# Keys, queries and x of two chunks in one tile, turned by one DMA transpose, and v loaded from SyncE's queue

## The chip, the core and the metric

The kernel runs on one core of a Trainium2 chip. The metric is the device time of one execution in microseconds (us); the median over 13 runs before the change is 304.58 us. A core has a matrix engine (TensorE, "PE" in the profile; its weight loads are listed as "PEld"), VectorE ("DVE"), ScalarE ("ACT"), GpSimd ("POOL") and SyncE ("SP"). Each engine works through its own instruction stream in order, and semaphores between the streams make one wait for another. SyncE computes nothing: its stream issues transfers. An issue is itself an instruction in a stream, so whatever stands behind a waiting issue waits too.

## The reference

```python
# q, k, v: (8 sequences, 8 heads, 576 positions, 64), float32
scores = scale * np.matmul(q, k.transpose(0, 1, 3, 2))
rel = pos[:, None] - pos[None, :]
mask = (rel >= 0) & (rel < 64)              # a causal window of 64 keys
scores = np.where(mask, scores, -1000000000.0)
attn = softmax(scores)                      # shortened here
x = np.matmul(attn, v)                      # then laid out as (4608 tokens, 512)
h = np.maximum(x @ w_in, 0.0)               # w_in: 512 x 2048
out = h * h @ w_out                         # w_out: 2048 x 512, out: 4608 x 512
```

Attention within a short window comes first, and a two-layer network with a squared ReLU follows it. Nearly all the arithmetic is in the two large products.

## The kernel before

**Tiles.** The 4608 tokens are 36 chunks of 128 tokens, and chunks 2p and 2p+1 are pair p. A sequence of 576 positions is two pairs of 256 and a rest of 64. The rests of all sequences are gathered in pairs 8 and 15 (`TAILS`): each of their four chunks holds the last 64 queries of two sequences, and needs 128 keys and values of each. Four chunks are a group g of 512 tokens, and there are nine groups.

**One chunk's way.** Rows of k, q and v are loaded as float32 into staging tiles (`fetch_rows`, L122), cast to float16 (`cast_k`, `cast_q`, `cast_v`, mostly on POOL, L264; the tails' at L301 and L304), and the keys and queries are turned so that the head dimension lies across partitions. The first 14 chunks are turned by PE (`T`, L330) and copied out of PSUM; from chunk 14 on SyncE issues a DMA transpose for each (`dma_kT` L357, `dma_tail` L363, `dma_qT` L368). `S_` (L388) makes the scores with the turned keys as weights, `expo` (L394) the exponential on ScalarE, `keep` (L399) the mask on DVE, `V` (L411) the product with v, and `norm` (L418, L419) divides by the row sum and writes x. x is turned too, by PE for groups 0 to 3 (`X`, L430), and by a DMA transpose of each chunk after that (`dma_xT`, L438).

The keys of a pair lie in one tile of 64 + 256 columns: a block of 64 query rows needs the 64 keys before it as well, so `halo` (L315, L317) has DVE fill the first 64 columns, with zeros at the start of a sequence or with the last 64 columns of the pair before.

**The network.** `UP(g, f)` (L489) makes one of 16 slices of h for a group; ScalarE takes the ReLU (L493), and either ScalarE (L496) or DVE (L499) squares it. There are two PSUM banks for these slices. `out_seven(g)` (L577) makes the second product with seven half-size products in place of eight; its half sums and differences are made by DVE (`hsum`, L565), its results leave PSUM at L592 to L599, and SyncE stores them (L608, L614).

**Order.** The first phase, some 80 us, is a list written by hand (`FIRST`). After it a loop runs over g = 2 to 9. Each turn puts the second product of group g-1, the first product of group g, the attention of group g+1 and the loads into one list with a time from 0 to 1 each, and issues them in the order of these times. In `loads`, a pair a = 2g+3 is turned from 0.06 on (its second chunk at 0.11), its halo is filled at 0.2, and the chunks two further on are loaded at 0.14 and 0.38; the second pair follows 0.46 later in the same way. `attention` has scores at 0.02 and 0.48, the product with v at 0.25 and 0.71, and the turning of x at 0.275 and 0.735.

**Queues.** All loads, stores and transposes are issued from SyncE, except for the v loads of chunks from `AHEAD` = 22 on, which are issued from ScalarE's stream (16 loads):

```python
fetch_rows(vv[:, n], v, b + n, S - 128, eng=nc.scalar if i >= AHEAD else nc.sync)
```

In the built program the transfers share eight completion counters, taken in turn, and an issue waits until the transfer eight places earlier has landed, whichever queue issued that one.

**Staging.** `two_tiles` hands out six tiles of two chunks each. A key and a query load of one chunk share one such tile; from chunk 22 on two v loads share one. POOL's casts free them. The float16 copies rotate through seven one-chunk tiles each for keys and queries, the turned queries through five, x through three.

Of the kernel before, what the change touches and what calls it, by code (L numbers as in the profile page):

```python
# [41 lines left out]
def kernel(  # L42
# [13 lines left out]
    P = 128  # L56
# [15 lines left out]
    st16 = ctx.enter_context(tc.tile_pool(name="st16", bufs=7))  # L72
# [66 lines left out]
    AHEAD = 22  # L139
# [4 lines left out]
    def fetch_kq(i, eng=nc.sync):  # L144
        st = two_tiles()
        sts["k", i], sts["q", i] = st[:, 0], st[:, 1]
        for nm, src in (("k", k), ("q", q)):
            fetch_rows(sts[nm, i], src, *place(i), eng=eng)

    def fetch_v(i, eng=nc.sync):  # L150
        if i < AHEAD:
            sts["v", i] = stage.tile([P, H, D], FP32, name="v_st", tag="st", bufs=5)
        elif i % 2 == 0:
            vv = two_tiles()
            sts["v", i], sts["v", i + 1] = vv[:, 0], vv[:, 1]
        fetch_rows(sts["v", i], v, *place(i), eng=eng)

    def fetch_tail(i):

        kk, vv = two_tiles(), two_tiles()  # L160
        if i % 2 == 0:
            qq = two_tiles()
            sts["q", i], sts["q", i + 1] = qq[:, 0], qq[:, 1]
        sts["k", i], sts["v", i] = (kk[:, 0], kk[:, 1]), (vv[:, 0], vv[:, 1])
        b = tail_seq(i)
        for n in range(2):
            fetch_rows(kk[:, n], k, b + n, S - 128)
        for n in range(2):
            fetch_rows(sts["q", i], q, b + n, S - 64, 64, 64 * n)
        for n in range(2):  # L170
            fetch_rows(vv[:, n], v, b + n, S - 128, eng=nc.scalar if i >= AHEAD else nc.sync)
# [80 lines left out]
    for name, m in (("minus_first", mask_first), ("minus_inner", mask_inner)):  # L252
        minus.append(const.tile([P, 512], FP16, name=name))
        nc.vector.tensor_scalar(out=minus[-1][:], in0=m[:].rearrange("p a r -> p (a r)"),
                                scalar1=-BIG, scalar2=None, op0=ALU.add)


    kTs, qTs, pms, xs, xTs = {}, {}, {}, {}, {}
# [8 lines left out]

    def cast_k(i, eng=nc.gpsimd):
        k16s[i] = st16.tile([P, H, D], FP16, name="k16", tag="k16")
        copy(eng, k16s[i][:], sts["k", i])  # L270

    def cast_q(i, eng=nc.gpsimd):
        q16s[i] = st16.tile([P, H, D], FP16, name="q16", tag="q16")
        copy(eng, q16s[i][:], sts["q", i])
# [18 lines left out]
    def xT_of(g):  # L293
        if g not in xTs:
            xTs[g] = xtp.tile([P, DMC, 512], FP16, name="xT", tag="xT")
        return xTs[g]

    def cast_tail(i):
        k16s[i] = [st16.tile([P, H, D], FP16, name="k16", tag="k16") for _ in range(2)]
        for n in range(2):  # L300
            nc.gpsimd.tensor_copy(out=k16s[i][n][:], in_=sts["k", i][n])  # L301
        cast_q(i)
        for n, vv in enumerate((v_ods, v_evs)):
            nc.gpsimd.tensor_copy(out=vv[i % NV][:, :, 0:D], in_=sts["v", i][n])  # L304

    def kT_of(p):

        if p not in kTs:
            kTs[p] = attw.tile([P, HP, 64 + 2 * P], FP16, name="kT", tag="kT", bufs=4)
        return kTs[p]  # L310

    def halo(i):
        p = i // 2
        if is_first(i):
            nc.vector.memset(kT_of(p)[:, :, 0:64], 0.0)  # L315
        else:
            nc.vector.tensor_copy(out=kT_of(p)[:, :, 0:64], in_=kT_of(p - 1)[:, :, 2 * P:2 * P + 64])  # L317

# [5 lines left out]
    def T(p):  # L324
        ps = att_bank("qkT_ps")[:].rearrange("p s f -> p (s f)").bitcast(FP16).rearrange(
            "p (s two a t) -> p s a two t", s=2, two=2, a=HP)
        for s, src in enumerate((k16s, q16s)):
            for n in range(2):
                for hp in range(HP):
                    nc.tensor.transpose(out=ps[:, s, hp, n, :],  # L330
                                        in_=src[2 * p + n][:, 2 * hp:2 * hp + 2, :],
# [6 lines left out]

    def q_cols(i):
        qTs[i] = attw.tile([P, HP, P], FP16, name="qT", tag="qT", bufs=5)  # L340
        return qTs[i][:]
# [14 lines left out]
    def dma_kT(i):  # L356
        nc.sync.dma_start_transpose(out=k_cols(i), in_=k16s[i][:].rearrange("p h d -> p (h d)"))  # L357

    def dma_tail(i):

        kTs["tail", i] = attw.tile([P, HP, 64 + 2 * P], FP16, name="kT", tag="kT", bufs=4)
        for n in range(2):
            nc.sync.dma_start_transpose(out=kTs["tail", i][:, :, n * P:(n + 1) * P],  # L363
                                        in_=k16s[i][n][:].rearrange("p h d -> p (h d)"))
        dma_qT(i)

    def dma_qT(i):
        nc.sync.dma_start_transpose(out=q_cols(i), in_=q16s[i][:].rearrange("p h d -> p (h d)"))  # L368

    def S_(i):  # L370
        sc = att_bank("sc")
        scv = sc[:].rearrange("p a (h b t) -> p a h b t", h=HP, b=2)
        for a in range(2 if i < 4 else 0):
            nc.tensor.matmul(sc[:, a, :], ident[:], minus[i > 0][:], start=True, stop=False,
                             skip_group_check=True)
        tail = is_tail(i)
        kT = kTs["tail", i] if tail else kT_of(i // 2)
        for hp in range(HP):
            for blk in range(2):
                for hh in range(2):  # L380
                    r0 = 64 * hh
                    k0 = P * blk if tail else i % 2 * P + 64 * blk
                    qT = qTs[i][r0:r0 + 64, hp, :]
# [4 lines left out]
                    nc.tensor.matmul(scv[:, hh, hp, blk, :], kT[r0:r0 + 64, hp, k0:k0 + P], qT,  # L388
# [26 lines left out]
    def norm(i):  # L415
        xs[i] = attw.tile([P, 2, HP, D], FP16, name="x_sb", tag="x_sb")
# [3 lines left out]
            out=xs[i][:], in0=avs[i][:, :, :, 0:D],  # L420
            in1=rden[:].to_broadcast([P, 2, 4, D]), op=ALU.mult)

    def xT_cols(i):
        return xT_of(i // 4)[:, :, (i % 4) * P:(i % 4 + 1) * P]

    def X(i):
        xps[i] = att_bank("xt_ps")[:, 0, :].bitcast(FP16)[:, 0:DMC * P].rearrange(
            "p (c t) -> p c t", c=DMC)
        for c in range(DMC):
            nc.tensor.transpose(out=xps[i][:, c, :],  # L430
                                in_=xs[i][:, c // 2, 2 * (c % 2):2 * (c % 2) + 2, :],
# [5 lines left out]
    def dma_xT(i):  # L437
        nc.sync.dma_start_transpose(out=xT_cols(i), in_=xs[i][:].rearrange("p a h d -> p (a h d)"))  # L438
# [16 lines left out]
    def U(p, j):  # L455
        t0 = p % 2 * 256
        pool, tag = either_pool()
        hps = pool.tile([P, 2, 256], FP32, name="hps2", tag=tag)
        for f in range(2):
            for c in range(DMC):  # L460
                nc.tensor.matmul(  # L461
                    hps[:, f, :], w_in_sb[:, c, (2 * j + f) * P:(2 * j + f + 1) * P],
                    xT_of(p // 2)[:, c, t0:t0 + 256], start=(c == 0), stop=(c == DMC - 1))
# [22 lines left out]
    def UP(g, f):  # L486
        hps = ps_up.tile([P, 512], FP32, name="hps", tag="ps_u")
        for c in range(DMC):
            nc.tensor.matmul(  # L489
                hps[:], w_in_sb[:, c, f * P:(f + 1) * P], xT_of(g)[:, c, :],  # L490
# [57 lines left out]
    def out_seven(g):  # L548
# [115 lines left out]
        "T": T, "ck": copy_kT, "cq": copy_qT, "tk": dma_kT, "tq": dma_qT, "h": halo,  # L664
        "S": S_, "e": expo, "ea": lambda i: expo(i, lo), "eb": lambda i: expo(i, hi),
        "m": keep, "ma": lambda i: keep(i, lo), "mb": lambda i: keep(i, hi),
        "V": V, "n": norm, "X": X, "x": copy_xT, "dx": dma_xT,
# [11 lines left out]
    def attention(g):  # L679
# [10 lines left out]
        def to_xT(i):  # L690
# [4 lines left out]
            else:  # L695
                dma_xT(i)
# [6 lines left out]
        for h in range(2):  # L703
# [3 lines left out]
                   (t + dx, lambda a=a: to_xT(a)), (t + dx + 0.001, lambda b=b: to_xT(b))]  # L707
        return ev

    def load(i):  # L710
        if is_tail(i):
            fetch_tail(i)
            cast_tail(i)
            return
        fetch_kq(i)
        fetch_v(i, nc.scalar if i >= AHEAD else nc.sync)
        cast_k(i)
        cast_q(i)
        cast_v(i)
        shift_v(i)  # L720

    def loads(c):

        ev = []
        for h in range(2):
            t = 0.46 * h
            for n in range(2):
                i = c + 2 * h + n
                if i < NCK:
                    ev.append((t + 0.06 + 0.05 * n, lambda i=i: dma_tail(i) if is_tail(i)  # L730
                               else (dma_kT(i), dma_qT(i))))
                if i < NCK and n == 0 and not is_tail(i):
                    ev.append((t + 0.2, lambda i=i: halo(i)))
                if i + 2 < NCK:
                    ev.append((t + 0.14 + 0.24 * n, lambda i=i: load(i + 2)))
# [5 lines left out]
    for g in range(2, NTB + 1):  # L741
# [6 lines left out]
        if g + 1 < NTB:  # L748
            ev += attention(g + 1)
            ev += loads(4 * g + 6)  # L750
# [34 lines left out]
```

## Time and profile before

| | |
|---|---|
| median of 13 runs | 304.58 us (303.31 to 306.59) |
| the profiled execution | 304.58 us |
| its span in the profile | 302.9 us |
| DMA busy, mean data rate | most of the time up to about 240 us; 190 GB/s |
| granted TensorE clock | 1.00 in every stretch looked at |

| group of instructions | count | mean |
|---|---|---|
| `UP` matmuls, 128x512 (L489) | 448 | 379 ns |
| ReLU of these on ScalarE (L493) | 112 | 597 ns |
| half sums and differences of h on DVE (L565) | 64 | 681 to 844 ns |
| casts of k, q on POOL (L264) | 40 | 729 to 757 ns |
| key transposes by DMA, landing after issue (L357, L363) | 26 | 3.8 us, median |
| query transposes by DMA (L368) | 22 | 2.6 us, median |
| x transposes by DMA (L438) | 20 | 4.0 us, median |
| k loads of one chunk, 256 KB | 26 | 4.2 us, median |

The profile shows one execution. Its span runs from the first instruction to the last. Matmuls overlap in PE's pipeline and their ends are modelled, so the time that PE takes for a matmul is the distance from one start to the next, which is shorter than the mean in the table: four matmuls of 512 columns start over 0.87 us. In lines of the timeline, the columns are the start in us, the time from the first start to the last end in us, the engine, the source line, the operation, what it writes and reads, the count, and in brackets how long the engine had been idle and what was seen to release it. "SPq" and "ACTq" are issues of transfers from the streams of SyncE and ScalarE.

### The profile page before, as it was taken

How to read it: one execution, taken by the hardware profiler on the slowest of the kernel's cores; microseconds unless marked ns; L12 is line 12 of the kernel's file. 1: busy time of each engine (PE TensorE's matmuls, PEld its weight loads, DVE VectorE, ACT ScalarE, POOL GpSimd, SP SyncE). 2: the span in 40 equal slices, each digit the busy share in tenths (PEclk: the TensorE clock that was granted, in tenths of full speed). 3: DMA queues.
4: the chain of work that ended last, by engine and by line, in shares of the span. 5: the costliest groups of instructions: out<-in, count | busy, mean ns of one | idle time of the engine just before them, and what ended most of it. 6: DMA issues, size and time to landing. Idle time of an engine off the chain costs nothing.

```text
span 302.9 us, 7559 instructions
## 1 busy us (share of the span) xinstructions
PE 285.6 (94%) x3026; PEld 197.1 (65%) x3026; DVE 214.5 (71%) x398; ACT 186.4 (62%) x303; POOL 121.4 (40%) x176
## 2 busy tenths in 40 slices
PE   1989999999999999999999999998989999999995
PEld 0658888855566676666666666665656666666685
DVE  4668888866878569775968596766575967646493
ACT  3558799795584756756675667475637675566510
POOL 1338955674605419263744566334263400000000
DMA  8999999896359779999997999999999911400133
GB/s 229 308 394 265 275 292 370 279 233 159 124 119 214 159 192 243 156 196 213 255 196 166 273 208 171 225 242 191 174 181 248 173 34 28 147 0 0 71 105 106
DMA packets 152931, 57.65 MB, mean 190 GB/s; under 512 B 129344, under 2 KB 144704, under 8 KB 152896
## 3 DMA queue, kind: packets, MB, share of 16 engines
q1 hardware_dynamic: 136256, 52.97, 72.1%
q10 hardware_dynamic: 16640, 4.20, 7.4%
q8 instruction: 24, 0.39, 0.5%
q14 instruction: 11, 0.09, 0.1%
HBM read 38.80 MB, written 9.44 MB: 159 GB/s over the span
## 4 chain that ended last, share of the span: by engine, by line
PE 64%; DVE 11%; DMA 10%; ACT 5%; SPq 4%; issue 3%; POOL 2%; ACTq 0%; POOLq 0%; DVEq 0%
PE hps L489 20%; PE hps L461 9%; PE opsC L577 7%; PE opsD L577 6%; DMA kq_st<-in_k_dram 6%; DVE hs_all L565 5%; PE ops L537 4%; PE opsB L577 3%; PE sc L388 3%; PE opsA L577 3%; DVE pm L399 3%; PE av L411 2%; PE qkT_ps L330 2%; ACT pm L394 2%; ACT hrelu L493 2%
## 5 line engine op out<-in xcount | busy, mean ns | idle before, releaser
L489 PE MATMUL hps<-xT,w_in_sb 128*128 128x512 f16 x448 | 112.9, 379 | 4.9 <-ACT hrelu L493 2.5
L493 ACT ACTIVATE hrelu<-hps 128x512 f32<-128x512 f32 x112 | 66.3, 597 | 73.9 <-PE hps L489 65.6
L577 PEld LDWEIGHTS <-h 128*128 128x128 f16 x624 | 60.4, 98 | 21.0 <-issue 0.2
L489 PEld LDWEIGHTS <-w_in_sb 128*128 128x128 f16 x448 | 42.8, 98 | 37.9 <-issue 5.4
L499 DVE SCALAR_TENSOR_TENSOR h<-hps,hrelu 128x512 f16<-128x512 f32 x56 | 38.6, 689 | 37.8 <-ACT hrelu L493 37.7
L264 POOL COPY v_od<-v_ev 64x512 f16<-64x512 f16 x52 | 36.6, 704 | 8.8 <-ACT v_ev L262 5.8
L394 ACT ACTIVATE pm<-sc 128x1024 f16<-128x1024 f32 (+1 forms) x40 | 35.6, 936 | 4.1 <-PE sc L388 3.9
L496 ACT ACTIVATE h<-hrelu 128x512 f16<-128x512 f32 x56 | 35.2, 629 | 1.6
L264 POOL CAST k<-kq_st 128x512 f16<-128x512 f32 x18 | 13.6, 757 | 48.2 <-DMA kq_st<-in_k_dram 47.9
L577 PE MATMUL opsA<-w_out_sb,h 128*128 128x256 f16 x240 | 31.0, 273 | 0.0
L577 PE MATMUL opsD<-wb_all,h 128*128 128x256 f16 x240 | 31.0, 273 | 0.0
L577 PEld LDWEIGHTS <-hs_all 128*128 128x128 f16 x256 | 25.0, 98 | 8.6
L461 PE MATMUL hps<-xT,w_in_sb 128*128 128x256 f16 x256 | 30.4, 273 | 0.0
L461 PEld LDWEIGHTS <-w_in_sb 128*128 128x128 f16 x256 | 24.1, 98 | 3.2 <-DVE w_in_sb L266 0.2
L419 DVE TENSOR_TENSOR x_sb<-av,rden 128x512 f16<-128x512 f32 x36 | 24.9, 691 | 1.2
L399 DVE TENSOR_TENSOR pm<-pm,mask_inner 128x1024 f16<-128x1024 f16 x25 | 19.8, 791 | 5.7 <-ACT pm L394 5.6
L264 POOL CAST q<-kq_st 128x512 f16<-128x512 f32 x22 | 16.0, 729 | 9.4 <-DMA kq_st<-in_q_dram 9.2
L388 PEld LDWEIGHTS <-kT 64*128 64x128 f16 x576 | 12.7, 95 | 7.6 <-issue 6.1
L577 PE MATMUL opsC<-w_out_sb,h 128*128 128x256 f16 x128 | 16.4, 273 | 0.0
L577 PE MATMUL opsC<-w_out_sb,hs_all 128*128 128x256 f16 x128 | 16.4, 273 | 0.0
L577 PE MATMUL opsB<-wb_all,hs_all 128*128 128x256 f16 x128 | 16.4, 272 | 0.0
L388 PE MATMUL sc<-qT,kT 64*128 64x64 f16 x576 | 15.9, 203 | 0.4 <-DVE qT L264 0.4
(97 smaller groups left out, 363.4 us busy)
## 6 DMA issues: line engine op xcount, KB each, us to landing
kq_st<-in_k_dram SPq DMA_DIRECT2D x26, 256.0 KB, 4.2
out_dram<-osb_all SPq DMA_DIRECT2D x12, 512.0 KB, 4.0
v_st<-in_v_dram SPq DMA_DIRECT2D x20, 256.0 KB, 4.9
kq_st<-in_q_dram SPq DMA_DIRECT2D x18, 256.0 KB, 4.3
kq_st<-in_v_dram ACTq DMA_DIRECT2D x16, 256.0 KB, 4.4
k_st<-in_k_dram SPq DMA_DIRECT2D x7, 512.0 KB, 5.4
q_st<-in_q_dram SPq DMA_DIRECT2D x7, 512.0 KB, 5.9
out_dram<-osb_all SPq DMA_DIRECT2D x11, 256.0 KB, 2.2
```

Of the source, the lines that this page charges most:

```text
L264: eng.tensor_copy(out=out, in_=in_)
L388: nc.tensor.matmul(scv[:, hh, hp, blk, :], kT[r0:r0 + 64, hp, k0:k0 + P], qT, start=i >= 4, stop=True, skip_group_check=i < 4)
L394: nc.scalar.activation(out=pms[i][:, part], in_=scs[i][:, part], func=AF.Exp, scale=1.0 / float(D) ** 0.5)
L399: nc.vector.tensor_tensor(out=pms[i][:, part], in0=pms[i][:, part], in1=mask[:].rearrange("p (o a) r -> p o (a r)", o=1) .to_broadcast([P, ...
L419: nc.vector.tensor_tensor(out=xs[i][:], in0=avs[i][:, :, :, 0:D], in1=rden[:].to_broadcast([P, 2, 4, D]), op=ALU.mult)
L461: nc.tensor.matmul(hps[:, f, :], w_in_sb[:, c, (2 * j + f) * P:(2 * j + f + 1) * P], xT_of(p // 2)[:, c, t0:t0 + 256], start=(c == 0), sto ...
L489: nc.tensor.matmul(hps[:], w_in_sb[:, c, f * P:(f + 1) * P], xT_of(g)[:, c, :], start=(c == 0), stop=(c == DMC - 1))
L493: nc.scalar.activation(out=hrelu[:], in_=hps[:], func=AF.Relu)
L496: later(2 if f == 0 else 0, lambda: nc.scalar.activation(out=h2_of(g)[:, f, :], in_=hrelu[:], func=AF.Square))
L499: nc.vector.scalar_tensor_tensor(out=h2_of(g)[:, f, :], in0=hps[:], scalar=0.0, in1=hrelu[:], op0=ALU.max, op1=ALU.mult)
L565: nc.vector.tensor_tensor(out=Sh[i][:, ks], in0=x[:, ks], in1=y[:, ks], op=op)
L577: nc.tensor.matmul(rows_of(bank, m), a[:, kk, m * P:(m + 1) * P], w[:, kk], start=(first and kk == 0 and (m == 0 or bank in apart)), stop= ...
```

## The change

All pairs from 7 on (`AHEAD` is now 7, counted in pairs) are handled as a whole. The float16 keys of a pair lie in one tile of two chunks, and so do its queries and its x; each of the three is turned by one DMA transpose of 1024 columns in place of two of 512. The staging tiles hold two chunks of one kind (k, q or v), and a pair's six loads (twelve for a tail pair) are issued one after the other at 0.14 and at 0.60 of a group, all from SyncE. The casts follow in the order k, k, q, q, v, v.

Since the transpose fills the turned tile from its first column, the keys have no room for the halo in front of them. `halo_apart`, at 0.30 and 0.76, has DVE build a second tile of 128 columns: the last 64 keys of the pair before (or zeros), and the first 64 of the pair itself. The first block of queries takes its keys from there.

x of a group is stored with the chunk outside and the column inside, so a matmul of `UP` reads its 512 columns as four runs of 128. The two constant masks `minus` now lie in an output tile that is not in use yet.

```diff
-    st16 = ctx.enter_context(tc.tile_pool(name="st16", bufs=7))
+    st16 = ctx.enter_context(tc.tile_pool(name="st16", bufs=3))
...
-    AHEAD = 22
+    AHEAD = 7
...
+    def fetch_two(nm, p):
+        src = {"k": k, "q": q, "v": v}[nm]
+        st = two_tiles()
+        b, s0 = place(2 * p)
         for n in range(2):
+            fetch_rows(st[:, n], src, b, s0 + n * P)
+        for n in range(2):
+            sts[nm, 2 * p + n] = st[:, n]
...
+    def halo_apart(p):
+        khs[p] = attw.tile([P, HP, P], FP16, name="kh", tag="kh", bufs=2)
+        if is_first(2 * p):
+            nc.vector.memset(khs[p][:, :, 0:64], 0.0)
+        else:
+            c0 = 2 * P if p - 1 < AHEAD else 2 * P - 64
+            nc.vector.tensor_copy(out=khs[p][:, :, 0:64], in_=kT_of(p - 1)[:, :, c0:c0 + 64])
+        nc.vector.tensor_copy(out=khs[p][:, :, 64:P], in_=kT_of(p)[:, :, 0:64])
...
-    def dma_kT(i):
-        nc.sync.dma_start_transpose(out=k_cols(i), in_=k16s[i][:].rearrange("p h d -> p (h d)"))
...
+    def dma_k(p):
+        if p in TAILS:
+            for i in (2 * p, 2 * p + 1):
+                kTs["tail", i] = attw.tile([P, 2, HP, P], FP16, name="kT", tag="kT", bufs=4)
+                flip(kTs["tail", i][:].rearrange("p n a t -> p (n a) t"),
+                     k16s["tail", i][:].rearrange("p n h d -> p (n h d)"))
+        else:
+            flip(kT_of(p)[:].rearrange("p a (n t) -> p (a n) t", n=2),
+                 k16s[p][:].rearrange("p n h d -> p (n h d)"))
+
+    def dma_q(p):
+        flip(qT_of(p)[:].rearrange("p n a t -> p (n a) t"),
+             q16s[p][:].rearrange("p n h d -> p (n h d)"))
...
-    def dma_xT(i):
-        nc.sync.dma_start_transpose(out=xT_cols(i), in_=xs[i][:].rearrange("p a h d -> p (a h d)"))
+    def dma_xT(p):
+        nc.sync.dma_start_transpose(
+            out=xT_of(p // 2)[:, p % 2 * 2:p % 2 * 2 + 2].rearrange("p n c t -> p (n c) t"),
+            in_=xs[p][:].rearrange("p n a h d -> p (n a h d)"))
...
-                hps[:], w_in_sb[:, c, f * P:(f + 1) * P], xT_of(g)[:, c, :],
+                hps[:], w_in_sb[:, c, f * P:(f + 1) * P], xT_of(g)[:, :, c, :],
...
+    def load(p):
+        if p in TAILS:
+            fetch_tail(p)
+        else:
+            for nm in "kqv":
+                fetch_two(nm, p)
+        for i in (2 * p, 2 * p + 1):
...
+                cast_k(i)
+        for i in (2 * p, 2 * p + 1):
+            cast_q(i)
...
-                if i + 2 < NCK:
-                    ev.append((t + 0.14 + 0.24 * n, lambda i=i: load(i + 2)))
+            t, a = 0.46 * h, p + h
+            if a < NCK // 2:
+                ev.append((t + 0.06, lambda a=a: (dma_k(a), dma_q(a))))
+                if a not in TAILS:
+                    ev.append((t + 0.3, lambda a=a: halo_apart(a)))
+            if a + 1 < NCK // 2:
+                ev.append((t + 0.14, lambda a=a: load(a + 1)))
```

## The prediction

> **What bounds the kernel now.** I read the page's busy times first, then the waits, then the timelines of PE, ScalarE and SyncE around the longest gaps. The page shows PE full and full speed granted:
>
> ```profile
> PE 285.6 (94%) x3026; PEld 197.1 (65%) x3026; DVE 214.5 (71%) x398; ACT 186.4 (62%) x303; POOL 121.4 (40%) x176
> ```
>
> So only what keeps PE from its next matmul counts. The timeline of PE, from 80 us on, has these gaps over 0.1 us (start, length, instruction, and in brackets the gap before it and its releaser):
>
> ```profile
> 102.78 1.02 PE L489 MATMUL hps<-xT,w_in_sb 128*128 128x512 f16 x4 [0.45 <-DVE h L499]
> ...
> 119.93 1.89 PE L489 MATMUL hps<-xT,w_in_sb 128*128 128x512 f16 x8 [0.60 <-DVE h L499]
> 133.86 1.02 PE L489 MATMUL hps<-xT,w_in_sb 128*128 128x512 f16 x4 [0.31 <-ACT hrelu L493]
> ...
> 178.53 1.89 PE L489 MATMUL hps<-xT,w_in_sb 128*128 128x512 f16 x8 [0.19 <-DVE h L499]
> ...
> 209.27 1.02 PE L489 MATMUL hps<-xT,w_in_sb 128*128 128x512 f16 x4 [0.84 <-ACT hrelu L493]
> 211.63 1.02 PE L489 MATMUL hps<-xT,w_in_sb 128*128 128x512 f16 x4 [0.46 <-DVE h L499]
> 219.58 1.89 PE L489 MATMUL hps<-xT,w_in_sb 128*128 128x512 f16 x8 [0.17 <-DVE h L499]
> 224.35 1.02 PE L489 MATMUL hps<-xT,w_in_sb 128*128 128x512 f16 x4 [1.38 <-ACT hrelu L493]
> ...
> 240.03 1.89 PE L489 MATMUL hps<-xT,w_in_sb 128*128 128x512 f16 x8 [0.31 <-DVE h L499]
> ```
>
> Five of them (0.31, 0.84, 0.46, 0.17, 1.38) make 3.16 us. The distance between the first opsA matmuls of successive groups agrees. They start at 112.44, 142.34, 171.45, 200.58, 232.83 and 261.40, so groups 3 to 7 take 29.90, 29.11, 29.13, 32.25 and 28.57 us (the last one starts a group without scores, 0.57 us, so 29.14 like for like). Group 6 is 3.1 us over the floor, group 3 is 0.8.
>
> What happens there is in the timeline of ScalarE, whose own queue issues the v loads (ACTq) between the ReLUs:
>
> ```profile
> 132.24 0.44 ACTq L122 DMA_DIRECT2D kq_st<-in_v_dram  x1
> 132.73 1.08 ACT L493 ACTIVATE hrelu<-hps 128x512 f32<-128x512 f32 x2 [1.98 <-DMA kq_st<-in_q_dram]
> ...
> 208.15 0.38 ACTq L122 DMA_DIRECT2D kq_st<-in_v_dram  x1
> 208.62 0.60 ACT L493 ACTIVATE hrelu<-hps 128x512 f32<-128x512 f32 x1 [3.62 <-PE hps L489]
> ...
> 214.76 0.37 ACTq L122 DMA_DIRECT2D kq_st<-in_v_dram  x1
> 215.23 0.60 ACT L493 ACTIVATE hrelu<-hps 128x512 f32<-128x512 f32 x1 [1.95 <-DVE u L599]
> ...
> 222.80 0.37 ACTq L122 DMA_DIRECT2D kq_st<-in_v_dram  x1
> 223.22 1.09 ACT L493 ACTIVATE hrelu<-hps 128x512 f32<-128x512 f32 x2 [3.26 <-DMA kT<-k]
> ```
>
> Each long ACT idle (1.98, 3.62, 1.95, 3.26) ends just after a v load goes out. The load waits, and the ReLU behind it waits too: in the built program a v load on ScalarE's queue waits for its staging tile and for the completion counter of the DMA eight places earlier, often a transpose that SyncE has yet to issue. The name in the bracket is only the last event seen; the 3.26 us one names such a transpose. A late ReLU frees its PSUM bank late and makes the square behind it late, and PE, with two such banks, stops.
>
> **The change, part by part.**
>
> *v loads leave ScalarE* (16 issues). The four blocks go, and with them the five gaps: -3.2 us. Group 6's excess (3.1) plus group 3's 0.31 would say 3.45; the listed gaps are the lower count and I take -3.3. Here the Trainium skill speaks against the change: "DMA: Bandwidth & Descriptors", section "Issuing engines are not separate DMA queues", says that spreading issues over engines only saves sequencer time for the issue, a small thing. By that rule the move gains ScalarE some 16 x 0.4 us of issue under cover and costs SyncE as much: about 0 in the sum, 304.6. The row differs: the issue takes 0.37 to 0.44 us, but it also waits in order, up to 3.62 us. The measurement decides.
>
> *SyncE's queue*, per steady group. Before: 8 key and query and 4 x transposes of 1.21 us, 8 loads of 0.57, 2 stores of about 0.6, which is 20.3 us without waits. After: 6 transposes of 1024 columns, 12 loads (6.8 us), 2 stores. No row shows a 1024-column transpose. Below: the 128x8x64 load that issues in 0.57 us however the rows are cut suggests a fixed part, so 0.57 + 2 x 0.64 = 1.85 us; above, it costs two old ones, 2.42. I take 1.85: 11.1 + 6.8 + 1.2 = 19.1 us; with 2.42 it is 22.5. Both fit in 29.1, so SyncE costs nothing as long as its order delays nobody. By hand for group 4 (start 141.4): key transposes from 142.4 after the second store (evacuated at 141.7), queries 144.3, six loads 146.3 to 150.0, x transposes at 151.1 (when the second x_sb is written), the next keys when their casts end (loads land some 4.5 us after issue, POOL casts 0.62 each) at 153.3, queries 155.3, six loads 157.2 to 161.0, x at 164.9, landed by 169 and first read at 172. Everything is in place with 3 us or more to spare. Before, the first key transpose of that group went out at 145.10, behind single loads. The tightest is group 5, where the tail pair brings twelve loads in a row (186 to 196) and the x transposes behind them go out about 196 and land near 200; the first UP of group 6 wants them at 201.5. Cost 0; with 2.42 us transposes it is late by about 1.5.
>
> *DVE's new wait.* The old halo copy (L317 and L315, 209 to 216 and 165 ns mostly) read an old key tile; `halo_apart` also reads the tile just being transposed, so DVE, in order, waits for that DMA. Nine pairs do it. It adds 9 copies of half the size (at most 9 x 0.22 = 2 us of DVE over 150 us, beside PE; DVE then idles 1.31 us before the square at 153.70). Queued behind it are the squares of UP and the h differences, and PE waits for those. A 512-column key transpose lands 2.3 to 5.6 us after issue. By the schedule above DVE reaches the copy at about 151.8 (keys out at 142.4) and 163.6 (keys out at 153.3): 9.4 and 10.3 us. If the double size adds 1 to 2 us to the landing, this is hidden: 0. If it doubled the worst, 11.2, it would start to show.
>
> *When POOL works.* Before, the second chunk of a pair was loaded late, and its casts fall at the start of the next group, beside the four half sums of DVE (L565 hs_all, mean 836 and 844 ns against 681 for h<-h of the same shape when POOL is quieter; in group 2, with POOL idle, they take 690). After, a pair's six casts follow one load at 0.14 and 0.60 of a group, so the start is quiet. The DVE gaps at group starts (0.60, 0.19, 0.31) are the cover: 0 to -1.1, I take -0.4. The casts then meet the h differences, where DVE has the 1.31 us of idle.
>
> *Strided x.* UP now reads x as 4 runs of 128 columns, not one of 512. Nothing shows that; the nearest row is the score matmuls: 32 take 1.09 us (83.64 to 84.73) in the chunks whose query columns jump at each element, 0.57 (111.87 to 112.44) where they don't, so 16 ns for 64 jumps, 0.25 ns each. Three jumps in 448 matmuls and one in 256 are 0.4 us above, 0 below: +0.2.
>
> *The rest*: the masks inside osb_all (its last load goes out at 46.35, long after chunk 3's scores), other buffer counts, tail casts of 1024 columns, and the first 80 us with the same instructions in the same order: 0, +0.1 for what I overlook. Their cover is that the new buffers (pairs, three deep) are written three pairs after their readers.
>
> Sum against the profiled execution: 302.9 - 3.3 - 0.4 + 0.2 + 0.1 = 299.5 us of span; that execution's own time was 304.58, so 1.68 lies around the span: 301.2. It is also the median of the 13 runs, so no shift.
>
> **Rivals.**
>
> *A. ScalarE's waits come back on SyncE, no net change.* With twelve loads at one point and the counter of the DMA eight before, SyncE stands still, and x reaches group 6 late. For: in the tails before, two 64-row query loads took up to 2.69 us to issue where 128-row ones take 0.57 each. Against: SyncE has 7 to 10 us free per group and no transpose is now waited for by another queue. If each of the twelve took 1.3 us, they would end at 202 and x would land at 206, 4.5 us late: 304.58 - 3.4 + 4.5 = 305.7 at worst. I take two thirds of that lateness, 3 us: 304.2, with 303.4 to 305.2 around it.
>
> *B. Slower: DVE held by `halo_apart`.* Place: 0.30 and 0.76 of each group from pair 9 on. It decides from the landing time: slack 9.4 to 10.3, plus the 1.31 us that DVE idles after it, about 11.1 us. Beyond it every us costs nine times; break-even with the gain of 3.4 is at 11.5, and at 11.8 us the time is 304.58 - 3.4 + 6.3 = 307.5. For: the double size, and all loads ahead of it in one queue. Against: 5.6 us is the longest now, in a busy time; key transposes follow loads that are already cast, so landed.
>
> *C. The transpose costs as two, or SyncE runs late at the tail only*: 302.7, inside the first case.
>
> **Chances.** First case (C included) 0.70, own range 299.8 to 303.5 (all DVE gaps gone and no strided cost, to C plus 0.8). A 0.12, B 0.18. A difference of 0.3% (0.9 us) is about what a measurement of this kernel can tell from no change. Faster 0.70, the same 0.11, slower 0.19. The range reaches to 305.3, past A's upper end, leaving B's bad part and a little below out.
>
> **What would show it.** No ACTq loads, and ACT waits for DMA gone; PE gaps at 209, 224 gone and group 6 near 29.2 us; transposes issued in 1.8 to 2.5 us and landing in under 8; hs_all near 0.69 us, h<-h slower; no DVE wait on a kT transpose. DVE waiting for kT with PE gaps after it would be B; PE or PEld waiting for xT at a group's start would be A; an L489 group of four over 0.87 us apart would make the strided read dearer than I say.

## The result, and the profile after

The changed kernel takes 301.38 us (median of 11 runs, 300.25 to 302.96). Beside it the kernel before took 305.09 us (48 runs), a ratio of 0.9882 with a 95% interval of 0.9859 to 0.9906. The profiled execution took 301.19 us, with a span of 299.3 us where that of before had 302.9.

The first line of the page with the busy times, and the `UP` matmuls (mean ns, then the idle time before them):

```profile
PE 285.4 (95%) x3026; PEld 196.8 (66%) x3026; DVE 211.4 (71%) x407; ACT 187.0 (62%) x303; POOL 114.9 (38%) x172
...
L533 PE MATMUL hps<-xT,w_in_sb 128*128 128x512 f16 x448 | 112.9, 379 | 1.3 <-ACT pm L434 1.0
```

PE does the same work and is the bound as before. A matmul of `UP` that reads x in four runs of 128 columns has the same mean, 379 ns, and four of them still start over 0.86 to 0.87 us. What went is idle time. The waits of ScalarE from 80 us on, before the change (what waited, for whom: us in total, times, longest), name a DMA twice and reach 3.6 us:

```profile
ACT hrelu L493 <- PE hps L489: 65.6, 81, 3.6
ACT hrelu L493 <- DMA kT<-k: 3.3, 1, 3.3
...
ACT hrelu L493 <- DMA kq_st<-in_q_dram: 2.0, 1, 2.0
ACT hrelu L493 <- DVE u L599: 1.9, 1, 1.9
```

The same view after:

```profile
ACT hrelu L537 <- PE hps L533: 67.9, 91, 1.6
ACT p L636 <- PE opsA L621: 3.1, 8, 1.1
ACT hrelu L537 <- DVE kh L341: 1.1, 1, 1.1
```

No DMA is among them, and the longest wait is 1.6 us. The PE timeline from 110 us on kept one pause over 0.3 us, at the start of group 6:

```profile
201.46 1.02 PE L533 MATMUL hps<-xT,w_in_sb 128*128 128x512 f16 x4 [0.96 <-ACT pm L434]
```

The bracket names ScalarE, but what is late is x: its transfer, issued at 196.17, landed at 201.32. Two further profiles of this kernel have the pause at the same place, 1.25 and 2.12 us long, and give the transfer itself as its end (the first of them):

```profile
201.96 1.02 PE L533 MATMUL hps<-xT,w_in_sb 128*128 128x512 f16 x4 [1.25 <-DMA xT<-x_sb]
```

The first `opsA` matmuls of groups 3 to 8 now start at 112.82, 141.69, 170.57, 199.45, 229.45 and 257.66:

| group | 3 | 4 | 5 | 6 | 7 | sum |
|---|---|---|---|---|---|---|
| before, us | 29.90 | 29.11 | 29.13 | 32.25 | 28.57 | 148.96 |
| after, us | 28.87 | 28.88 | 28.88 | 30.00 | 28.21 | 144.84 |

These five groups give 4.12 us; the stretch before group 3 takes 0.38 more and that from group 8 on 0.14 more, which makes the 3.6 us of the span. The 0.38 is within what single executions differ by: in the profiles of this document group 2, which the change does not touch, starts anywhere from 80.70 to 82.78 us.

SyncE's timeline around the start of group 4 before the change (start, length, and what is issued):

```profile
145.10 1.56 SPq L357 DMA_TRANSPOSE kT<-k  x1
146.76 1.21 SPq L368 DMA_TRANSPOSE qT<-q  x1
```

And over group 4 after it (L397 turns keys and queries, L480 x):

```profile
141.57 1.54 SPq L397 DMA_TRANSPOSE kT<-k  x1
143.22 1.25 SPq L397 DMA_TRANSPOSE qT<-q  x1
144.52 1.21 SPq L122 DMA_DIRECT2D kq_st<-in_k_dram  x2
145.78 1.91 SPq L122 DMA_DIRECT2D kq_st<-in_q_dram  x2
147.74 2.39 SPq L122 DMA_DIRECT2D kq_st<-in_v_dram  x2
150.22 2.23 SPq L480 DMA_TRANSPOSE xT<-x_sb  x1
152.55 1.25 SPq L397 DMA_TRANSPOSE kT<-k  x1
153.91 1.25 SPq L397 DMA_TRANSPOSE qT<-q  x1
```

A transpose of 1024 columns issues in 1.24 us where nothing else holds it, and one of 512 columns took 1.21 us. That is the main number of this case: by these shortest issues, the half of the transposes that the merge removes is half of their issue time. The experiments show what it pays for.

### The profile page after: what moved, and what is told of

Same layout as the page of the kernel before. It is cut to its first block, busy times and chain, and to the rows that moved or that the text cites. A ratio compares the mean times of both kernels' runs of the same rounds, so it can differ in the third digit from the quotient of the medians.

```text
span 299.3 us, 7455 instructions
## 1 busy us (share of the span) xinstructions
PE 285.4 (95%) x3026; PEld 196.8 (66%) x3026; DVE 211.4 (71%) x407; ACT 187.0 (62%) x303; POOL 114.9 (38%) x172
## 4 chain that ended last, share of the span: by engine, by line
PE 91%; ACT 3%; DVE 2%; DMA 2%; issue 1%; SPq 0%; DVEq 0%
PE hps L533 32%; PE opsC L621 9%; PE hps L505 9%; PE opsA L621 9%; PE opsD L621 8%; PE opsB L621 5%; PE sc L428 4%; PE ops L581 4%; PE av L451 4%; PE qkT_ps L366 2%; DMA q_st<-in_q_dram 2%; PE xt_ps L471 1%; ACT pm L434 1%; PE sc L417 1%; PE warm L552 1%; ACT kT L270 1%
## 5 line engine op out<-in xcount | busy, mean ns | idle before, releaser
L543 DVE SCALAR_TENSOR_TENSOR h<-hps,hrelu 128x512 f16<-128x512 f32 x56 | 38.6, 690 | 31.9 <-ACT hrelu L537 31.6
L272 POOL COPY v_od<-v_ev 64x512 f16<-64x512 f16 x52 | 34.5, 664 | 12.5 <-ACT v_ev L270 9.5
L272 POOL CAST k<-kq_st 128x512 f16<-128x512 f32 x18 | 11.7, 650 | 48.4 <-DMA kq_st<-in_k_dram 48.3
L439 DVE TENSOR_TENSOR pm<-pm,mask_inner 128x1024 f16<-128x1024 f16 x25 | 18.5, 740 | 4.7 <-ACT pm L434 4.5
L272 POOL CAST q<-kq_st 128x512 f16<-128x512 f32 x22 | 15.0, 686 | 8.4 <-DMA kq_st<-in_q_dram 8.4
L643 DVE SCALAR_TENSOR_TENSOR osb_all<-opsD,u 128x512 f32<-128x512 f32 x14 | 9.7, 691 | 11.3 <-PE opsD L621 11.3
L459 DVE RECIPROCAL rden<-av 128x8 f32<-128x8 f32 x36 | 7.3, 202 | 13.9 <-PE av L451 13.8
```

Source lines behind the costliest of these rows:

```text
L272: eng.tensor_copy(out=out, in_=in_)
L439: nc.vector.tensor_tensor(out=pms[i][:, part], in0=pms[i][:, part], in1=mask[:].rearrange("p (o a) r -> p o (a r)", o=1) .to_broadcast([P, ...
L543: nc.vector.scalar_tensor_tensor(out=h2_of(g)[:, f, :], in0=hps[:], scalar=0.0, in1=hrelu[:], op0=ALU.max, op1=ALU.mult)
```

## The experiments

Every ratio below is to runs of the kernel before made beside the experiment. The experiments that start from the changed kernel are named so.

### The two parts, each alone

The first takes the kernel before and does the one thing that I had credited with nearly all of the gain: the v loads go to SyncE.

```diff
-            fetch_rows(vv[:, n], v, b + n, S - 128, eng=nc.scalar if i >= AHEAD else nc.sync)
+            fetch_rows(vv[:, n], v, b + n, S - 128)
...
-        fetch_v(i, nc.scalar if i >= AHEAD else nc.sync)
+        fetch_v(i)
```

> The kernel before, with its 16 v loads issued from SyncE and nothing else changed. My theory (the v issues block ScalarE, worth 3.2 to 3.4 us of the 3.7 us gained): 0.989 to 0.991 of the time before, about 301.5 us; the gaps at ScalarE of 2 to 3.6 us and the PE gaps of groups 3 and 6 gone, group 6 near 29.2 us. Rival 1 (the gain comes from loading by pairs and fewer transposes): 1.00, the gaps stay in another place. Rival 2 (SyncE's queue, with 12 transposes and 12 loads per group, is now too full): 1.00 or above, x late at group starts.

Measured: 313.34 us, ratio 1.0279 (1.0234 to 1.0325). ScalarE's blocks were gone and the kernel was 2.8% slower: my theory missed, and rival 2 came in. SyncE's timeline, in two pieces:

```profile
146.65 1.57 SPq L357 DMA_TRANSPOSE kT<-k  x1
148.33 1.21 SPq L368 DMA_TRANSPOSE qT<-q  x1
149.63 2.01 SPq L357 DMA_TRANSPOSE kT<-k  x1
151.74 1.21 SPq L368 DMA_TRANSPOSE qT<-q  x1
...
176.52 1.41 SPq L357 DMA_TRANSPOSE kT<-k  x1
```

Between 116 and 171 us no pause over 0.3 us is left between SyncE's issues; the kernel before had 1.32 us of them and the changed one has 14.1 us, counted issue by issue. Nor does SyncE wait for completion counters there: from 80 us on, every issue of this run found its counter free for at least 3.1 us, by the landing of the transfer that used it before. The stream is full of issues. The key transposes that open a group start at 117.25, 146.65 and 176.52, so SyncE needs 29.4 and 29.9 us for a group that PE does in 29. It falls behind a little in each group, and when the tail pair's loads come, PE stops for x and then for the queries:

```profile
206.11 1.81 PE L489 MATMUL hps<-xT,w_in_sb 128*128 128x512 f16 x4 [4.58 <-DMA xT<-x_sb]
...
223.36 0.61 PE L388 MATMUL sc<-qT,kT 64*128 64x64 f16 x16 [3.04 <-DMA qT<-q]
```

Group 6 takes 40.1 us there (200.48 to 240.57) in place of 32.25.

The converse keeps the changed kernel, its pairs and its merged transposes, and puts v of the pairs from 11 on back on ScalarE:

```diff
-            fetch_rows(st[:, n], src, b, s0 + n * P)
+            fetch_rows(st[:, n], src, b, s0 + n * P,
+                       eng=nc.scalar if nm == "v" and p >= 11 else nc.sync)
...
-                        fetch_rows(st[:, n], src, b + n, S - 128)
+                        fetch_rows(st[:, n], src, b + n, S - 128,
+                                   eng=nc.scalar if nm == "v" and p >= 11 else nc.sync)
```

> The kernel after, with the v loads of pairs 11 to 17 issued from ScalarE again, right behind the k and q loads in the order of the list. My theory: ScalarE waits again for staging tiles or for the transfer eight places earlier, 1 to 4 us at some of the seven places, and 1.5 to 4 us of the gain are lost: 0.994 to 1.001 of the time before. Rival 1 (pairs are what counts): within 0.3 us of the kernel after, 0.988.

Measured: 306.45 us, ratio 1.002 (0.9992 to 1.0049): no difference from before that can be told. Its profile has one block, at the tail pair's four v loads, in ScalarE's timeline:

```profile
187.41 5.91 ACTq L122 DMA_DIRECT2D kq_st<-in_v_dram  x4
193.37 1.09 ACT L539 ACTIVATE hrelu<-hps 128x512 f32<-128x512 f32 x2 [5.48 <-DMA kq_st<-in_v_dram]
```

PE pauses 3.81 us behind it. The groups without that block take 28.88 us, as in the changed kernel. The profiled execution was the shortest of the twelve, 303.38 us, and the only one with a mean granted clock of 1.00. The other eleven, which have no trace, took 305.36 to 308.26 us with a mean clock of 0.983 to 0.994. At 0.989, the value of most, I estimate 0.011 x 304.6 = 3.4 us of lost clock, about what separates the median from the profile.

So the four cells are, with the ratio to before in brackets because the times come from different batches:

| | v on ScalarE | v on SyncE |
|---|---|---|
| transposes of 512 columns, chunk by chunk | 305.3 (1, before) | 313.34 (1.0279) |
| transposes of 1024 columns, pair by pair | 306.45 (1.002) | 301.38 (0.9882) |

Neither part, taken whole, gains anything alone. The v loads need room on SyncE, and the merge makes it. The loss in the lower left cell comes from one place, the tail pair; the last experiment shows what is left of it when those four loads alone move.

### Is it the number of transposes, or the pairs?

The changed kernel with each transpose of 1024 columns issued as two of 512; all else stays.

```diff
     def flip(out, in_):
-        nc.sync.dma_start_transpose(out=out, in_=in_)
+        for n in range(2):
+            nc.sync.dma_start_transpose(out=out[:, 4 * n:4 * n + 4], in_=in_[:, 512 * n:512 * n + 512])
...
-        nc.sync.dma_start_transpose(
+        flip(
             out=xT_of(p // 2)[:, p % 2 * 2:p % 2 * 2 + 2].rearrange("p n c t -> p (n c) t"),
```

> The kernel after, with each transpose of 1024 columns issued as two of 512 into the same tiles. The profile after shows an issue of 1.24 us at least for 1024 columns, as for 512 before, so the merge saves some 1.3 us of SyncE for each of 33. My theory (SyncE has time to spare outside the tail): at most 0.5 to 1 us slower than the kernel after, from x reaching group 6 later. Rival (the merge is what made room for the v loads): 2 us or more slower, gaps at several group starts.

Measured: 327.25 us, ratio 1.0629 (1.0573 to 1.0686), 24.3 us more than the changed kernel beside it (302.96). I had expected 1 us at most; the rival came in. SyncE again has no pause between 116 and 171 us; its group takes 31.9 us (key transposes at 118.42 and 150.35):

```profile
150.35 3.49 SPq L398 DMA_TRANSPOSE kT<-k  x2
153.94 2.52 SPq L398 DMA_TRANSPOSE qT<-q  x2
```

And PE waits for x at four group starts, 20.4 us in all and 8.8 us at the longest, by its view of waits:

```profile
PE hps L534 <- DMA xT<-x_sb: 20.4, 4, 8.8
```

This is an upper end for what the merge alone is worth, because the order of the changed kernel was laid out for fewer issues. Each extra transpose also takes one of the eight completion counters, but the trace shows no wait for them: wherever the landing is recorded, SyncE's issues from 80 us on found their counter free for at least 2.5 us. Part of the 24 us is the granted clock, which fell to 0.5 around the three longest of these waits and stayed there for 4.1, 2.8 and 5.3 us after PE had gone on; at half rate I estimate that at 6 us. That SyncE has half as many transposes to issue is what the rest of the change stands on.

### The quiet start of a group

I had put 0.4 us down to POOL's casts no longer running beside DVE's half sums. Two runs were meant for it. The first is the run with v on SyncE, with both chunks of a pair loaded at once, early:

```diff
-                    ev.append((t + 0.14 + 0.24 * n, lambda i=i: load(i + 2)))
+                    ev.append((t + 0.14 + 0.001 * n, lambda i=i: load(i + 2)))
```

> The kernel before, v loads on SyncE, and both chunks of a pair loaded at 0.14 and 0.60 of a group (one after the other, still a tile and two 512-column transposes for each chunk). Theory of the quiet group start (POOL's casts move away from the half sums, worth about 0.25 us in each of groups 3 to 7): 1.0 to 1.5 us less than the same kernel without the early load; hs_all near 0.69 us in the mean instead of 0.84. If the paired transposes matter and not the time of the load: no difference from it.

Measured: 322.04 us, ratio 1.0513 (1.0456 to 1.057). This run says nothing on POOL: SyncE was full already, x came late three times (15.1 us of PE waiting, 6.5 at the longest), and that covers anything else. The half sums did not even become shorter (862 and 800 ns).

The second takes the changed kernel and loads a pair later, so that its casts fall into the next group's start:

```diff
-                ev.append((t + 0.14, lambda a=a: load(a + 1)))
+                ev.append((t + 0.38, lambda a=a: load(a + 1)))
```

> The kernel after, with the load of a pair at 0.38 and 0.84 of a group in place of 0.14 and 0.60. Theory of the quiet group start: casts on POOL fall on the half sums again, hs_all above 0.8 us in the mean, group length about 29.1 instead of 28.88, so 1 to 1.5 us slower than the kernel after (0.992 to 0.993 of before). Rival (late loads hurt through late keys): more than 2 us slower, with DVE waiting for a kT transpose at the halo copies.

Measured: 307.45 us, ratio 1.007 (1.0044 to 1.0096). The half sums, by form, before the change, in the changed kernel and in this one (the last number before the final bar is the mean in ns):

```profile
L565 DVE TENSOR_TENSOR hs_all<-hs_all,h 128x1024 f16<-128x1024 f16 x16 | 13.5, 844 | 0.6
L565 DVE TENSOR_TENSOR hs_all<-h 128x1024 f16<-128x1024 f16 x16 | 13.4, 836 | 0.0
```

```profile
L609 DVE TENSOR_TENSOR hs_all<-hs_all,h 128x1024 f16<-128x1024 f16 x16 | 11.1, 692 | 0.6
L609 DVE TENSOR_TENSOR hs_all<-h 128x1024 f16<-128x1024 f16 x16 | 10.9, 682 | 0.0
```

```profile
L609 DVE TENSOR_TENSOR hs_all<-hs_all,h 128x1024 f16<-128x1024 f16 x16 | 14.1, 882 | 0.6
L609 DVE TENSOR_TENSOR hs_all<-h 128x1024 f16<-128x1024 f16 x16 | 13.8, 863 | 0.0
```

The trace ties this to POOL, instruction by instruction. Of the 32 half sums, 18 ran with POOL busy at some time before the change, none in the changed kernel, and 18 again here. All the half sums and differences that had POOL idle beside them took 676 to 693 ns in these three runs; each that took over 720 ns (up to 1407) had POOL busy for at least 43% of its time.

With the longer half sums the pauses behind DVE's square are back at the starts of groups, as before the change (0.19, 0.62 and 0.61 us, at 120, 150 and 243 us), and groups 3 and 4 take 29.13 and 29.56 us where the changed kernel takes 28.87 and 28.88 (group 5, which has no such pause, takes 28.87 in both within 0.01). So the quiet start is real. It is not most of this run's loss: a single wait for queries in group 6, which were loaded late too, costs 4.58 us and a stretch of slower matmuls.

```profile
218.25 1.04 PE L428 MATMUL sc<-qT,kT 64*128 64x64 f16 x32 [4.58 <-DMA qT<-q]
```

### The halo that waits for the transpose

The strongest case against the change was DVE, held in order by `halo_apart` until the keys' transpose has landed. Here the transposes of keys and queries are issued at 0.22 rather than 0.06, and the halo stays at 0.30:

```diff
-                ev.append((t + 0.06, lambda a=a: (dma_k(a), dma_q(a))))
+                ev.append((t + 0.22, lambda a=a: (dma_k(a), dma_q(a))))
```

> The kernel after, with the key and query transposes at 0.22 of a group and 0.68, behind the loads of the next pair and just ahead of the halo copies at 0.30 and 0.76. This measures rival B of the prediction, DVE held by the copy: the keys now leave SyncE some 4 to 6 us later, so DVE should wait 1 to 4 us for the transpose at each of nine copies. If DVE's slack there is about 1.3 us, the time is 3 to 15 us above the kernel after; if it is within 0.5 us of it, the copies have far more room than I worked out.

Measured: 314.08 us, ratio 1.0208 (1.0168 to 1.0248); the changed kernel in the same batch took 302.96 us (0.9837, 0.9789 to 0.9885). The wait appears in DVE's view of waits (19.4 us, six times), and the longest of them stops PE through x, which DVE writes behind the halo:

```profile
DVE kh L342 <- DMA kT<-k: 19.4, 6, 6.6
```

```profile
100.13 0.61 PE L471 MATMUL xt_ps<-ident,x_sb 128*128 128x128 f16 x4 [4.74 <-DVE x_sb L460]
```

By the start of group 3 this kernel is already 8.7 us behind (121.55 against 112.82). In SyncE's timeline, the keys went out there at 94.47, behind a tail pair's twelve loads, while DVE stood at the halo from 91.8 to 98.4. The mechanism is therefore real and dear. In the changed kernel no DVE wait for a key transpose is listed: the keys go out early enough and land in at most 6.4 us.

```profile
L397 SPq DMA_TRANSPOSE kT<-k x13: 1236/1413/2727, 82.7 to 229.3; - x13
...
DMA to landing us min/median/max: 2.8/4.3/6.4
```

### The remaining pause

In the changed kernel x of group 6 goes out late, behind the twelve loads of the tail pair (lengths of 3.2 to 4.0 us are for four loads):

```profile
185.40 4.04 SPq L122 DMA_DIRECT2D kq_st<-in_k_dram  x4
189.49 3.21 SPq L122 DMA_DIRECT2D kq_st<-in_q_dram  x4
192.74 3.33 SPq L122 DMA_DIRECT2D kq_st<-in_v_dram  x4
196.17 3.09 SPq L480 DMA_TRANSPOSE xT<-x_sb  x1
```

The next kernel moves pair 15's four v loads and their casts from 0.60 to 0.75 of the group:

```diff
-            fetch_tail(p)
+            fetch_tail(p, "kq" if p == 15 else "kqv")
...
+                if a + 1 == 15:
+                    ev.append((t + 0.29, lambda: load_tail_v(15)))
```

> The kernel after, with the four v loads of the second tail pair (15) moved from 0.60 to 0.75 of group 5, behind the x transpose. The kernel after has one PE gap of 0.96 us at the start of group 6, which I put down to x being issued at 196.17 us behind twelve loads. If so the gap shrinks to under 0.3 us and the time is 0.7 to 1 us below the kernel after (0.985 to 0.986 of before). If the gap is from something else: no change.

> The kernel after as it is, on the same chip as the next three: 0.988 of the time before.

Measured: 301.2 us, ratio 0.9788 (0.9744 to 0.9833), beside 0.9837 (0.9789 to 0.9885) for the changed kernel run with it. The pause at group 6 is gone (28.94 us), and one of 0.82 us at the start of group 7 stands in its place, for x again:

```profile
230.71 1.02 PE L533 MATMUL hps<-xT,w_in_sb 128*128 128x512 f16 x4 [0.82 <-DMA xT<-x_sb]
```

So the load of pair 17, which comes before that x, was moved in the same way:

```diff
-                ev.append((t + 0.14, lambda a=a: load(a + 1)))
+                ev.append((t + (0.29 if a + 1 == 17 else 0.14), lambda a=a: load(a + 1)))
```

> The kernel after, with the tail's v loads behind the x transpose of group 5 and the last pair's six loads behind the x transpose of group 6 (0.75 in place of 0.60). Moving the tail's v alone closed the gap at the start of group 6 (group length 28.94 us) but opened one of 0.82 us at the start of group 7, where x had come late behind the next loads. My theory (each x transpose is late by what stands ahead of it on SyncE): both gaps gone, 1 us below the kernel after, 0.980 to 0.984 of before. Rival: the last pair's keys now come late, PE waits for qT near the middle of group 7, and nothing is gained.

> The kernel after as it is, as the mark for the next two: 0.984 to 0.988 of the time before.

Measured: 300.89 us (300.53 to 301.02), ratio 0.9853 (0.9814 to 0.9892), beside 301.34 us (300.30 to 303.45), 0.9875 (0.9829 to 0.9921), for the changed kernel. Both pauses are gone: x goes out at 193.04 and 221.73 and issues in 1.2 to 1.3 us, and groups 3 to 6 take 28.88, 28.87, 28.88 and 28.88 us.

```profile
193.04 1.30 SPq L480 DMA_TRANSPOSE xT<-x_sb  x1
...
221.73 1.23 SPq L480 DMA_TRANSPOSE xT<-x_sb  x1
```

A pause of 0.48 us behind DVE's square, at 235.72, is new in this run, and its group 7 takes 28.75 us where the changed kernel's takes 28.21. The medians are 0.45 us apart and the intervals overlap, so this is not shown to be faster. The six runs lie within 0.5 us, and the changed kernel's within 3.2.

The last one asks whether, with the tail's v on SyncE and late, the other v loads from pair 11 on could go back to ScalarE:

```diff
-            fetch_rows(st[:, n], src, b, s0 + n * P)
+            fetch_rows(st[:, n], src, b, s0 + n * P,
+                       eng=nc.scalar if nm == "v" and p >= 11 else nc.sync)
```

> The kernel after, with the v loads of pairs 11 to 17 on ScalarE except those of the tail pair 15, which SyncE issues behind the x transpose of group 5. With all of them on ScalarE there was one block, at the tail (5.48 us of ScalarE idle, a PE gap of 3.81), and nothing in other groups. My theory: once merged transposes keep SyncE on time, a v load on ScalarE hardly waits, so this runs as the kernel after or up to 1 us below it (0.981 to 0.988 of before), with no ScalarE idle over 1.5 us before a ReLU. Rival (v issues on ScalarE cost by themselves): 1 us or more above the kernel after.

Measured: 301.69 us (12 runs), ratio 0.9904 (0.9868 to 0.994). One block is left behind v loads, of 2.77 us where I had allowed none over 1.5, and PE pauses 0.46 us after it:

```profile
206.10 0.60 ACT L538 ACTIVATE hrelu<-hps 128x512 f32<-128x512 f32 x1 [2.77 <-PE av L452]
```

The interval overlaps that of the changed kernel (0.9875), so no difference is shown. With merged transposes the place of these loads matters little; what cost most in the second experiment was the tail pair's four in a row on ScalarE. So the merge, with those four loads moved, gains without the other v loads leaving ScalarE.

## Why the prediction was right, and where it was not

The time was forecast at 301.2 us and is 301.38. The parts were less exact than the sum, so that the sum is this close is in part luck: two misses of opposite sign, DVE's pauses and x of group 6, largely cancel. Measured on the same listing of PE's pauses:

| step of the prediction | forecast, us | measured, us |
|---|---|---|
| five pauses behind ScalarE's v loads go | -3.3 | -3.16, all gone |
| three pauses behind DVE at group starts (0.60, 0.19, 0.31) | -0.4 | -1.10, all gone |
| x read in four runs | +0.2 | 0 (379 ns and 379 ns) |
| x of group 6 late behind twelve loads | 0 | +0.96 |
| what the listing leaves out, groups 3 to 7 | not named | -0.82 |
| before group 3 and from group 8 on | +0.1 | +0.52 |
| sum | -3.4 | -3.6 |

**v loads leave ScalarE.** The blocks and the pauses went as said, and the trace of before bears out how they arose: each of the four loads went out 0.02 to 0.17 us after the landing of the transfer that had used its counter last. But my sum treated this as a gain of the move, and the run with v on SyncE shows that the move by itself loses 8 us (313.34 against 305.3). It pays only where SyncE has room. The prediction weighed this move against the Trainium skill's page "DMA: Bandwidth & Descriptors" (section "Issuing engines are not separate DMA queues"), by which issuing from several engines saves only the sequencer's time to initiate a transfer, usually small; I had priced that at about nothing. The runs bear out neither that price nor my way of setting it aside. The same move costs 2.8% with the old transposes and gains 1.4% with the new ones (1.002 for the second experiment against 0.9882 for the changed kernel, from different batches). Here the waits in an in-order stream, and how full that stream is, decide.

**SyncE's queue.** This is the step that failed, in its reasons and not in its sum. "Both fit in 29.1, so SyncE costs nothing", and with transposes of 2.42 us a delay of 1.5 us and 302.7 us in all: the run with two issues in place of one took 327.25 (302.96 for the changed kernel beside it). I had summed the shortest issues that the trace shows. In the timeline a load costs 0.57 us only when nothing holds it; the first six loads of group 4 take 1.21, 1.91 and 2.39 us in twos, 0.92 each. A wait for the counter of the transfer eight places before is not the cause on SyncE: in the changed kernel each of its issues from 80 us on found the counter free for at least 1.8 us. Its loads took 0.57 us in the median with at most two transfers under way and 0.85 with three or more; what makes them longer was not tried. By my sum the kernel before left SyncE 9 us free per group; the timeline had 1.32 us in 55. The second error had the other sign: a transpose of 1024 columns takes 1.24 us, below my lower bound of 1.85, for I let the issue grow with the columns. Had it cost what my upper bound says, the split run suggests a loss of some 6%, far from case C. The hand-made times for the starts in group 4 nevertheless came within 2.0 us, and SyncE was the earlier each time: keys at 141.57 (forecast 142.4), the first loads at 144.52 (146.3), x at 150.22 (151.1), the second keys at 152.55 (153.3), the second loads at 155.21 (157.2).

**The tail (rival A).** "The tightest is group 5": x was to go out about 196, to land near 200, and to be wanted at 201.5. It went out at 196.17, held SyncE until 199.26 and landed at 201.32, and the matmul that reads it started at 201.46, 0.96 us after PE had become free. So the place was right and the cost of zero was not; rival A came in at a third of the 3 us that I gave it.

**DVE's new wait (rival B).** Hidden, as forecast, with landings of at most 6.4 us where some 11 us were allowed. The run with later transposes is 11.1 us slower (314.08 against 302.96), most of it from this mechanism (8.7 us of the profiled execution are lost by the start of group 3; late queries cost it more later on); I had made it the case that ends on the other side, and rightly.

**POOL.** Under-sized: all three pauses went, which was the far end of the range that I gave, and by the starts of the matmuls the term is -1.5. `hs_all` fell from 844 and 836 to 692 and 682 ns. The casts did meet the h differences, as said: of those, one form went from 681 to 758 ns and the other from 808 to 732, with no pause of PE behind them.

**What the listing leaves out.** It counts a pause from a modelled end, so I took the distance from one start to the next in the trace instead. From the last matmul of the product with v to the next `UP` it is 0.12 us where nothing waits. Before the change it was 0.80, 0.34, 0.38 and 0.50 us at 119.93, 149.41, 178.53 and 240.03, each time released by DVE's square: 1.5 us too much in all. The one at 149.41 is the excess of group 4 (29.11 us, now 28.88), which had no pause in the listing: it is 0.15 us from the modelled end, and the listing starts above that, not at 0.1. Counted in the same way, ScalarE's five pauses are 3.8 us and the late x of group 6 is 1.1, and 3.8 + 1.5 - 1.1 is the gain of groups 3 to 7 (4.12) within 0.1 us.

**What stays open.** What makes an issue on SyncE longer than its shortest, and where the clock fell in the executions of the second experiment that have no trace.

## What to carry to other kernels

Price a queue's stream by the pauses left between its issues over the stretch that matters, not by the sum of its shortest issues: SyncE looked 70% used and had 1.3 us free in 55. When an issue blocks a computing engine, moving it is only half a change; first make room where it goes, and merging transposes does this where one of double width issues in the same time. When a burst of loads stands before a transfer that the bounding engine needs next, move the part of the burst that nobody wants soon, and look for the pause at the next such place.

## What was not expected of the hardware

**The issue of a DMA transpose did not depend on its width here.** At the shortest it was 1.19 us for 128x512 (x, before the change) and 1.23 us for 128x1024 (x, after it) in float16, both from SyncE. The landing of the keys went from 2.3, 3.8 and 5.6 us (shortest, median, longest) to 2.8, 4.3 and 6.4; in the split run the narrow ones landed in 2.5 us in the median, so other work in the queue has its part in these times. No other widths were run.

**A long pause of PE costs more than itself, but not always.** In the windows of the run with v on SyncE, after the 4.58 us wait for x (the columns from the left: window, its length, the busy time with the number of instructions of PE, PEld, DVE, ACT and POOL, then the granted clock, the DMA share and GB/s):

```profile
206.00:209.00 3.00, 2.89 (x11) 1.50 (x12) 0.49 (x1) 0.60 (x1) 0.00 (x0) 0.54 0.86 198
209.00:212.00 3.00, 3.00 (x19) 1.90 (x18) 0.66 (x1) 1.60 (x3) 0.98 (x2) 0.89 1.07 242
```

The same view of the run with merged transposes and v on ScalarE, after its pause of 3.81 us:

```profile
194.00:197.00 3.00, 2.50 (x16) 1.56 (x16) 2.93 (x7) 1.68 (x3) 0.73 (x2) 1.00 1.11 246
```

From 80 us on, the clock fell to half after pauses of 2.25, 3.04, 3.59, 4.58 (twice), 4.63, 4.74, 4.96, 6.21, 6.53 and 8.80 us in these runs, and stayed full after this one of 3.81 and after one of 2.12 in the changed kernel. (In the other executions of the run with the 3.81 it probably fell, by their mean clock of 0.983 to 0.994.) The Trainium skill's page "TensorE: Matmul & The Clock Gate" (section "Part 1: The HAM clock gate (the "warmup" mystery)") gives half rate after an idle window of about 3.4 us, and a window that runs free of the kernel, so that a pause a little longer than the window need not contain a whole one. That agrees with the 3.81; but 3.04 and 2.25 are shorter than a window and the clock fell all the same (0.50 from 224 to 226 us in the run with v on SyncE, and from 226 to 228 in the run with late transposes), so the figure is no safe limit here. At half rate, 3 us do the work of 1.5, and the low stretches lasted about 3 to 6 us after PE had gone on: I estimate 1.5 to 3 us for each such pause on top of its own length. In the run with late loads this fits: group 6 took 35.08 us, 6.2 more than the 28.88 of a group without a wait, for a pause of 4.58. That is why single late transfers cost the experiments more than the pauses listed.
